# Summing a router's row blocks in PSUM by thirds of the tokens, and even static capacities, in a fused attention and mixture-of-experts kernel

## The chip, the cores and the metric

One Trainium2 chip, one of its cores. The metric is device microseconds of one execution, lower is better. The kernel before takes 606.49 us (median of three runs, 604.68 to 609.28).

## The reference, cut to what matters

Windowed attention for 8 batches, 8 heads, 576 positions and head size 64 gives a table x of 4608 tokens by 512 features. A two-level router then picks one of 16 experts for each token, and the token goes through that expert's two layers:

```python
g_logits = x @ w_group                 # 4 groups
g_idx = np.argmax(g_logits, axis=1)
...
    e_logits = xg @ w_expert[g]        # 4 experts in each group
    e_idx = np.argmax(e_logits, axis=1)
    ...
            h = np.maximum(xg[mask_e] @ w1[g, e], 0.0)     # 512 -> 1024
            ye = h @ w2[g, e]                              # 1024 -> 512
            out[tok_idx] = combined[:, None] * ye
```

So the router needs 20 numbers for each token: 4 group logits and 16 expert logits, each a sum over 512 features. On this input the reference sends 442, 405, 368, 301, 299, 298, 291, 284, 265, 264, 255, 255, 242, 238, 213 and 188 tokens to the sixteen experts, in the order in which the kernel ranks them.

## The kernel before, in words

**Attention.** The tokens are handled in 4 pairs of batches (1152 tokens each), and each pair in 9 steps, 36 steps in all. A step loads its queries, keys and values by DMA from SyncE's queue (tiles qb, kr, vt), computes scores on TensorE (PE; L266, L278), their maxima and differences on VectorE (DVE; L288, L289), the exponentials on ScalarE (ACT; L294), turns them (L301), multiplies by the values (tile o, L311), divides (L337, L339), stores x to DRAM and turns x into xT (L363, L365, L367). POOL (GpSimd) makes a shifted copy of the values (L125, L131). PE, ACT, DVE and SyncE run in the order in which the program writes their instructions; POOL's order is made by a planner.

**Router.** When the 9 steps of a pair are done, `route` runs for it, a piece at a time between later attention steps (`spend` with its budget). xT has the 512 features as 4 row blocks c of 128 partitions. In the kernel before, the 1152 tokens are cut into three thirds of 384. For each third, four products (one for each row block c) write four different 32-partition blocks of one PSUM tile lt_ps (L380), so the four partial sums lie under one another; the middle third is cut in two because it spans two batches. ACT copies each third to SBUF (tile lt, L387). In the next attention step, nine products, one for each 128-token tile, take a 128x128 block of lt as the stationary operand and a 128x20 matrix `sumsel` of ones and zeros as the moving one: that turns the tile and adds the four partial sums at once (tile lg_ps, L391). VectorE then finds the maxima (L396 and on), and a long chain gives each token a slot in its expert's list, ending in products into tb_ps (L521) and an addition to `tab` (L531). Float32 products on PE show as two records each, so 36 products of L391 are 72 records.

**The last pair's route** runs in the tail after the attention, in an order written out by hand (the string TAIL), between the first, early pieces of the expert layers. There `overflow`, `order` and `select` find the lists of rows, and POOL gathers rows of x for the experts (L700).

**Experts.** The experts are ranked by their number of tokens, and the rank r has a static capacity CAPS[r]: the layers are computed for that many columns, whatever the number of tokens. Parts of ranks 0 and 1 are done early (128+128 and 256 columns). For the rest, `layer1` does 8 blocks of 12 products (L750) in which the token columns are the moving operand, and `layer2` does 24 products for each tile of 128 tokens (L809) in which the weights move, 512 columns at a time; a last tile of at most 64 tokens is done in 2 groups side by side, one of at most 32 in 4. `spread` turns the gathered rows (L731). Tokens over a capacity are handled by a loop at the end of the program, once for each 128 of them, with its own load of the expert's weights; on this input it runs zero times.

Of the kernel before, what the change touches and what calls it, by code (L numbers as in the profile page):

```python
# [8 lines left out]
F32 = mybir.dt.float32  # L9
# [4 lines left out]
ALU = mybir.AluOpType  # L14
# [3 lines left out]
P = 128  # L18
B, H, S, D = 8, 8, 576, 64
# [7 lines left out]
TPB = 2 * S // P  # L27
# [9 lines left out]
CLS = S // 4  # L37
EARLY = ((0, 0, 128, 2), (0, 128, 128, 3), (1, 0, 256, 3))
AFTER = (2, 3)
CAPS = (448, 408, 368, 304, 304, 304, 296, 288, 272, 264, 256, 256, 248, 240, 216, 192)  # L40
DONE = [max([o + n for q, o, n, _ in EARLY if q == r] + [0]) for r in range(len(CAPS))]
PIECES = [(r, DONE[r], n - DONE[r]) for r, n in enumerate(CAPS)]
CMAX = max(n for _, _, n in PIECES)
# [21 lines left out]
def moe_attention_kernel(ctx, tc, q, k, v, cmask, wgate, wpack, out):  # L65
    nc = tc.nc
    pool = lambda name, bufs=1, **kw: ctx.enter_context(tc.tile_pool(name=name, bufs=bufs, **kw))
    cp = pool("cp")
    dram = pool("dram", space=bass.MemoryType.DRAM)
    psS = pool("psS", 2, space=PSUM)  # L70
    psT = pool("psT", 2, space=PSUM)
    psX = pool("psX", 1, space=PSUM)
    psR = pool("psR", 1, space=PSUM)
# [4 lines left out]
    id32 = cp.tile([P, P], F32, name="id32")  # L78
# [13 lines left out]
    sm = pool("sm", 1)  # L92
# [61 lines left out]
    upper = cp.tile([P, P], BF16, name="upper")  # L154
    wgr = cp.tile([P, 128 + NCHK], F32, name="wgr")
    wg = wgr[:, 0:128].rearrange("p (c n) -> p c n", c=4)
    sumsel = cp.tile([P, 20], F32, name="sumsel")
    pri = cp.tile([P, 4], F32, name="pri")
    base = [cp.tile([P, NE], F32, name="base0")] + [None] * NBP
    low = cp.tile([P, P], F32, name="low")  # L160
# [19 lines left out]
    def iota_of(t, pattern, base, mult):  # L180
        nc.gpsimd.iota(t, pattern=pattern, base=base, channel_multiplier=mult, allow_small_or_imprecise_dtypes=True)

    def setup(part):
        if part == 0:
            nc.vector.memset(ones, 1.0)
            nc.gpsimd.affine_select(
                out=upper, in_=ones, pattern=[[1, P]], compare_op=ALU.is_gt, fill=0.0, base=0, channel_multiplier=-1
            )
            nc.sync.dma_start(wgr, wgate)
            nc.vector.tensor_copy(sumsel, id32[:, 0:20])  # L190
            for c in range(1, 4):
                nc.vector.tensor_tensor(sumsel, sumsel, id32[:, 32 * c : 32 * c + 20], ALU.add)
            iota_of(pri, [[-1, 4]], 4, 0)
            iota_of(base[0], [[REG, NE]], 0, 0)
            iota_of(low, [[1, P]], 0, 0)
        if part == 1:
            iota_of(val[:, :, 0], [[P, NCHK]], -NTOK, 1)
            iota_of(parts[:, :, 0], [[P, NCHK]], -NTOK, 0)
            iota_of(parts[:, :, 3], [[0, NCHK]], 0, 1)
            iota_of(high, [[REG // P, NE], [1, NK4]], 0, 0)  # L200
            nc.vector.tensor_scalar(high, high, float(P), HUGE, ALU.mult, ALU.add)
            nc.vector.memset(E16, 0.0)
            nc.vector.memset(tab[:, 0], float(NTOK))
            nc.vector.memset(tab[:, 1], 0.0)
            nc.vector.memset(tab[:, 2], 2.0 * NTOK + 1.0)
            nc.vector.tensor_copy(val[:, :, 2], wgr[:, 128:])
            nc.vector.tensor_scalar(parts[:, :, 2], val[:, :, 2], R256, R256, ALU.add, ALU.subtract)
            nc.vector.tensor_tensor(parts[:, :, 5], val[:, :, 2], parts[:, :, 2], ALU.subtract)
        if part == 2:
            for t in sum(xe, []):  # L210
                nc.gpsimd.memset(t, 0.0)
            nc.sync.dma_start(xd[NTOK : NTOK + 1, :], xe[0][0][0:1, :])
        if part == 3:
            for g, t in oob.items():
                for i in range(g):
                    nc.gpsimd.memset(t[P // g * i : P // g * i + P // g], float(g * NTOK + i))
            for r in range(NE):
                nc.vector.memset(capt[:, r : r + 1], float(CAPS[r]))

# [134 lines left out]
    xT = {}  # L354
# [13 lines left out]


    def route(bp):  # L370
        lt = sm.tile([P, TPB, P], F32, name="lt")
        TPC = TPB // 3
        for i in range(3):
            ps = (psT, psT, psR)[i].tile([P, TPC * P], F32, name="lt_ps", tag="ttr"[i])
            a0 = i * TPC * P
            cuts = [a0] + [S] * (a0 < S < a0 + TPC * P) + [a0 + TPC * P]
            for a, b in zip(cuts, cuts[1:]):
                bb, s0, n = a // S, a % S, b - a
                for c in range(4):
                    nc.tensor.matmul(  # L380
                        ps[32 * c : 32 * c + 32, a - a0 : b - a0],
                        wg[:, c],
                        xT[bp][:, c, bb, s0 : s0 + n],
                        start=True,
                        stop=True,
                    )
            nc.scalar.copy(lt[:, i * TPC : i * TPC + TPC].rearrange("p t n -> p (t n)"), ps)  # L387
        yield 2
        lg_ps = psR.tile([P, TPB, 20], F32, name="lg_ps", tag="r")
        for t in range(TPB):  # L390
            nc.tensor.matmul(lg_ps[:, t], lt[:, t], sumsel, start=True, stop=True)  # L391
        n, last = TPB, bp + 1
        T = lambda nm, shape, dt=F32: sm.tile([P] + shape, dt, name=nm)
        l5 = lg_ps.rearrange("p t (r e) -> p t r e", e=4)
# [50 lines left out]
        for t in range(n):  # L445
# [4 lines left out]
                start=False,  # L450
                stop=(t == n - 1),
# [32 lines left out]
        for t0 in range(0, n, 3):  # L484
# [33 lines left out]
            for t1, lo, hv in done:  # L518
                for t in range(3):
                    for h in range(2):  # L520
# [4 lines left out]
                            start=(t1 + t + h == 0),  # L525
                            stop=(t1 + t == n - 1 and h == 1),
# [239 lines left out]
    def layer2(w, ent, cs, cap, between=lambda i: None, tail=None):  # L766
# [34 lines left out]
        if tl[-1][1] < P:  # L801
            tl.insert(0 if cap == CAPS[-1] else 1, tl.pop())
        for k, (t, n) in enumerate(tl):
# [80 lines left out]
    start = []  # L884
# [5 lines left out]
    for s in range(NT + 3):  # L890
# [13 lines left out]
        if start:  # L904
            n = start.pop()
            routes.append(route(n))
            for i, (_, _, _, pairs) in enumerate(EARLY):
                if pairs == n + 1:
                    routes.append(settle(i))
# [11 lines left out]
        if 2 <= s <= 8 and s % 2 == 0:  # L921
            setup(s // 2 - 1)
# [14 lines left out]
        if s >= 3 and (s - 3) % NJ == NJ - 1:  # L937
            bp = (s - 3) // NJ
# [122 lines left out]
    def ready():  # L1061
        cur[:] = begin(0)

    lastr = [route(NBP - 1)]
    bgq = [overflow()]
    rq = [order()]
# [138 lines left out]
```

## Time and profile before

| | us |
|---|---|
| median of three runs | 606.49 |
| profiled execution, whole | 609.38 |
| its span, first to last instruction | 607.7 |
| PE busy | 571.0 (94%) |
| DVE busy | 395.1 (65%) |
| ACT busy | 329.5 (54%) |
| POOL busy | 247.7 (41%) |

The profiled execution took 609.38 us, 2.9 us over the median of the runs. "Busy" is the union of an engine's instructions. PEld is TensorE's loading of stationary operands, which runs beside its products. The granted clock of TensorE is given as a share of full speed, so 1.00 is 2.4 GHz and 0.50 is 1.2 GHz.

### The profile page before, as it was taken

The page shows a single profiled execution, that of the slowest core. Times are in us where ns is not written, and L with a number is a line of the kernel's source. Part 1 is how long each engine was busy: PE and PEld are TensorE (multiplying, and loading weights), DVE is VectorE, ACT ScalarE, POOL GpSimd, SP SyncE. Part 2 cuts the span into 40 slices and gives each one's busy share as a digit, 9 for nine tenths or more (in the row PEclk, how much of TensorE's full clock was granted, in tenths as well). Part 3 has the DMA queues.
Part 4 walks back from the last instruction along what each step waited for, and adds up shares of the span by engine and source line. Part 5 has one row for each costly group of instructions (what it writes and reads, how often), then busy time and mean ns, then how long its engine had stood idle before and what let it go on. Part 6 is the DMA issues. An engine that isn't in the chain of part 4 may idle for free.

```text
span 607.7 us, 18716 instructions
## 1 busy us (share of the span) xinstructions
PE 571.0 (94%) x7636; PEld 400.4 (66%) x7636; DVE 395.1 (65%) x800; ACT 329.5 (54%) x658; POOL 247.7 (41%) x314
## 2 busy tenths in 40 slices
PE   5898999988879999999999999999999999999995
PEld 3665776666666668665666575666757767767873
DVE  5764874897957853774778786655755666656720
ACT  2555674675566533774465555465655756656521
POOL 4754582655726324143425151433524413413411
PEclk9999998989989999999999999999999999999999
DMA  7998796799374118676567576757668578677300
GB/s 245 298 287 262 238 277 185 237 356 335 71 250 144 51 47 318 219 259 205 183 198 223 187 229 205 226 175 232 209 211 258 180 243 275 227 233 254 103 30 29
DMA packets 47914, 127.52 MB, mean 210 GB/s; under 512 B 7224, under 2 KB 8126, under 8 KB 47826
## 3 DMA queue, kind: packets, MB, share of 16 engines
q1 hardware_dynamic: 40466, 105.31, 54.9%
q0 software_dynamic: 7360, 20.98, 9.8%
q8 instruction: 62, 1.02, 0.7%
q14 instruction: 26, 0.21, 0.1%
HBM read 107.38 MB, written 19.24 MB: 208 GB/s over the span
## 4 chain that ended last, share of the span: by engine, by line
PE 65%; issue 3%; DVE 2%; POOL 1%; ACT 1%; POOLq 0%
PE y L809 31%; PE a L750 30%; PE pt L731 3%; DVE mv L502 1%; POOL xe L700 1%; PE tb_ps L521 0%; POOL out L770 0%; PE rp L676 0%; ACT off L246 0%; DVE room L758 0%; ACT xT L367 0%; ACT ohl L247 0%; PE o L311 0%; ACT room L757 0%; DVE room L733 0%
## 5 line engine op out<-in xcount | busy, mean ns | idle before, releaser
L700 POOL DMA_INDIRECT xr<-xd,sent x80 | 96.1, 1201 | 35.2 <-issue 22.2
L809 PEld LDWEIGHTS <-hh 128*128 128x128 f16 (+10 forms) x960 | 67.5, 99 | 58.0 <-issue 2.9
L770 POOL DMA_INDIRECT out<-yr,sent x30 | 30.2, 1007 | 180.2 <-ACT yr L783 148.0
L758 DVE SCALAR_TENSOR_TENSOR hl<-a,hh 128x256 f16<-128x256 f32 (+11 forms) x136 | 57.3, 424 | 65.9 <-ACT hh L757 64.8
L757 ACT ACTIVATE hh<-a 128x256 f16<-128x256 f32 (+11 forms) x136 | 51.9, 385 | 51.9 <-PE a L750 51.2
L750 PE MATMUL a<-xh,wb1h 128*128 128x256 f16 (+6 forms) x288 | 77.0, 271 | 0.0
L750 PE MATMUL a<-xl,wb1h 128*128 128x256 f16 (+6 forms) x288 | 77.0, 271 | 0.0
L750 PE MATMUL a<-xh,wb1l 128*128 128x256 f16 (+6 forms) x288 | 77.0, 271 | 0.0
L733 DVE TENSOR_TENSOR xl<-pt,xh 128x512 f16<-128x512 f32 (+10 forms) x42 | 24.8, 594 | 73.5 <-ACT xh L732 73.5
L750 PE MATMUL a<-xh,wa1h 128*128 128x192 f16 (+7 forms) x256 | 71.2, 278 | 0.0
L750 PE MATMUL a<-xh,wa1l 128*128 128x192 f16 (+7 forms) x256 | 71.2, 278 | 0.0
L750 PE MATMUL a<-xl,wa1h 128*128 128x192 f16 (+7 forms) x256 | 71.2, 278 | 0.0
L783 ACT ACTIVATE yr<-y,cs 128x512 f32<-128x512 f32 (+3 forms) x30 | 20.6, 687 | 90.1 <-PE y L809 61.9
L750 PEld LDWEIGHTS <-wa1h 128*128 128x128 f16 x640 | 59.3, 98 | 13.4 <-issue 1.8
L750 PEld LDWEIGHTS <-wb1h 128*128 128x128 f16 x576 | 54.4, 98 | 10.0
L809 PE MATMUL y<-wb2h,hh 128*128 128x512 f16 (+6 forms) x272 | 59.7, 305 | 0.0
L809 PE MATMUL y<-wb2l,hh 128*128 128x512 f16 (+6 forms) x272 | 59.6, 304 | 0.0
L809 PE MATMUL y<-wb2h,hl 128*128 128x512 f16 (+6 forms) x272 | 59.6, 304 | 0.0
L809 PE MATMUL y<-wa2h,hh 128*128 128x512 f16 (+7 forms) x208 | 56.8, 332 | 0.0
L809 PE MATMUL y<-wa2l,hh 128*128 128x512 f16 (+7 forms) x208 | 56.6, 330 | 0.0
L809 PE MATMUL y<-wa2h,hl 128*128 128x512 f16 (+7 forms) x208 | 56.6, 330 | 0.0
L809 PEld LDWEIGHTS <-hl 128*128 128x128 f16 (+10 forms) x480 | 34.6, 99 | 25.2
(190 smaller groups left out, 1255.4 us busy)
## 6 DMA issues: line engine op xcount, KB each, us to landing
w<-wpack SPq DMA_DIRECT2D x128, 512.0 KB, 3.9
vt<-v SPq DMA_DIRECT2D x36, 260.0 KB, 4.8
qb<-q SPq DMA_DIRECT2D x36, 256.0 KB, 4.6
xd<-x SPq DMA_DIRECT2D x72, 128.0 KB, 3.9
kr<-k SPq DMA_DIRECT2D x34, 256.0 KB, 4.4
xr<-xd,sent POOLq DMA_INDIRECT x80, 4.1
kr<-k SPq DMA_DIRECT2D x4, 128.0 KB, 3.2
out<-yr,sent POOLq DMA_INDIRECT x30, 2.8
```

The costliest lines, as they stand in the source:

```text
L502: nc.vector.scalar_tensor_tensor(mv[:, t], high.rearrange("p e k -> p (e k)").unsqueeze(1).broadcast_to([P, 6, NE * NK4]), hl[:, 1, t0 + t ...
L700: nc.gpsimd.indirect_dma_start(out=xr[:, 256 * h : 256 * h + 256], out_offset=None, in_=xd[0:known].rearrange("n (h c) -> (n h) c", h=2), ...
L731: nc.tensor.transpose(pt[:, c, 0:n], xr[0:n, c * P : c * P + P], id32[0:n, 0:n])
L733: nc.vector.tensor_tensor(xl[:, :, t * P : t * P + n], pt[:, :, 0:n], xh[:, :, t * P : t * P + n], ALU.subtract)
L750: nc.tensor.matmul(a[:, 0:cap], ww[:, c * FF + f * P : c * FF + f * P + P], xx[:, c, 0:cap], start=(i == 0), stop=(i == len(mm) - 1),)
L757: nc.scalar.activation(hh[:, f, 0:cap], a[:, 0:cap], AF.Relu)
L758: nc.vector.scalar_tensor_tensor(hl[:, f, 0:cap], a[:, 0:cap], 0.0, hh[:, f, 0:cap], ALU.max, ALU.subtract)
L770: ins = nc.gpsimd.indirect_dma_start(out=out.rearrange("n (g c) -> (n g) c", g=g), out_offset=bass.IndirectOffsetOnAxis(ap=at, axis=0), in ...
L783: nc.scalar.activation(yr[0:n, :], yp[0:n, :], AF.Copy, scale=cs[0:n, t : t + 1])
L809: nc.tensor.matmul(yp[P // g * j : P // g * j + n, 0 : DM // g], h[:, f, t * P : t * P + n], ww[:, f * DM + DM // g * j : f * DM + DM // g ...
```

## The change

It does two things. In `route`, the three thirds now go to three 32-partition blocks of one PSUM tile, and the four row blocks c are added in PSUM by accumulation, so one copy of 96 partitions takes the place of three of 128. A product of the next stage then turns three token tiles (one of each third) at once, with a 96x60 selection matrix `sel3` in place of the 128x20 `sumsel`: three products in place of nine. And the capacities go from multiples of eight to the next even number; twelve of them shrink, by 48 columns in all.

```diff
-CAPS = (448, 408, 368, 304, 304, 304, 296, 288, 272, 264, 256, 256, 248, 240, 216, 192)
+CAPS = (442, 406, 368, 302, 300, 298, 292, 284, 266, 264, 256, 256, 242, 238, 214, 188)
...
-    sumsel = cp.tile([P, 20], F32, name="sumsel")
+    sel3 = cp.tile([P, 3, 20], F32, name="sel3")
...
-            nc.vector.tensor_copy(sumsel, id32[:, 0:20])
-            for c in range(1, 4):
-                nc.vector.tensor_tensor(sumsel, sumsel, id32[:, 32 * c : 32 * c + 20], ALU.add)
+            for j in range(3):
+                nc.vector.tensor_copy(sel3[:, j], id32[:, 32 * j : 32 * j + 20])
...
     def route(bp):
-        lt = sm.tile([P, TPB, P], F32, name="lt")
         TPC = TPB // 3
-        for i in range(3):
-            ps = (psT, psT, psR)[i].tile([P, TPC * P], F32, name="lt_ps", tag="ttr"[i])
-            a0 = i * TPC * P
-            cuts = [a0] + [S] * (a0 < S < a0 + TPC * P) + [a0 + TPC * P]
-            for a, b in zip(cuts, cuts[1:]):
-                bb, s0, n = a // S, a % S, b - a
-                for c in range(4):
+        lt = sm.tile([3 * 32, TPC * P], F32, name="lt")
+        ps = psT.tile([P, TPC * P], F32, name="lt_ps", tag="t")
+        for c in range(4):
+            for j in range(3):
+                a0, a1 = j * TPC * P, (j + 1) * TPC * P
+                cuts = [a0] + [S] * (a0 < S < a1) + [a1]
+                for a, b in zip(cuts, cuts[1:]):
+                    bb, s0 = a // S, a % S
                     nc.tensor.matmul(
-                        ps[32 * c : 32 * c + 32, a - a0 : b - a0],
+                        ps[32 * j : 32 * j + 32, a - a0 : b - a0],
                         wg[:, c],
-                        xT[bp][:, c, bb, s0 : s0 + n],
-                        start=True,
-                        stop=True,
+                        xT[bp][:, c, bb, s0 : s0 + b - a],
+                        start=(c == 0 and a == a0),
+                        stop=(c == 3 and b == a1),
                     )
-            nc.scalar.copy(lt[:, i * TPC : i * TPC + TPC].rearrange("p t n -> p (t n)"), ps)
+        nc.scalar.copy(lt, ps[0 : 3 * 32])
         yield 2
         lg_ps = psR.tile([P, TPB, 20], F32, name="lg_ps", tag="r")
-        for t in range(TPB):
-            nc.tensor.matmul(lg_ps[:, t], lt[:, t], sumsel, start=True, stop=True)
+        for t in range(TPC):
+            nc.tensor.matmul(
+                lg_ps.rearrange("p (j t) e -> p j t e", t=TPC)[:, :, t],
+                lt[:, t * P : t * P + P],
+                sel3[0 : 3 * 32],
+                start=True,
+                stop=True,
+            )
```

## Rows read from the trace of the kernel before

**Rows 1.** Busy time by stage (start:end, length, then each engine's busy time), clock, DMA.
```profile
core 0: us, PE busy (x) PEld busy (x) DVE busy (x) ACT busy (x) POOL busy (x), PEclk, DMA share, GB/s
...
20.00:180.00 160.00, 139.46 (x3788) 104.37 (x3787) 117.48 (x252) 96.87 (x247) 86.48 (x138) 0.95 0.80 249
180.00:230.00 50.00, 47.74 (x433) 33.43 (x433) 33.71 (x94) 24.84 (x57) 20.12 (x26) 1.00 0.28 94
...
300.00:400.00 100.00, 100.00 (x776) 65.21 (x775) 72.79 (x150) 53.10 (x90) 37.27 (x33) 1.00 0.65 205
```

**Rows 2.** Chain that ended last: start, us, what; first layer at 304 and 264 columns.
```profile
295.58 6.20 PE a L750 x48
...
455.17 5.40 PE a L750 x48
```

**Rows 3.** Timeline of PE, 300 to 350: turning of a full tile and of 48 rows.
```profile
313.32 0.60 PE L731 MATMUL pt<-id,xr 128*128 128x128 f32 x4
...
317.28 0.45 PE L731 MATMUL pt<-id,xr 48*128 48x48 f32 x4
```

**Rows 4.** Groups by line (busy, mean ns): the router's products, loads and copies.
```profile
L380 PE MATMUL lt_ps<-xT,wgr 128*32 128x384 f32 (+1 forms) x128 | 9.4, 410 | 1.1 <-issue 0.9
L391 PE MATMUL lg_ps<-sumsel,lt 128*128 128x20 f32 x72 | 9.3, 275 | 0.0
L391 PEld LDWEIGHTS lg_ps<-sumsel,lt 128*128 128x128 f32 x72 | 8.9, 201 | 0.4
...
L387 ACT COPY lt<-lt_ps 128x384 f32<-128x384 f32 x12 | 5.7, 479 | 4.4 <-PE lt_ps L380 4.1
```

**Rows 5.** Line L380 alone, 182.5 to 182.7 and 183.3 to 183.6: min/median/max ns.
```profile
L380 PE MATMUL lt_ps<-xT,wgr x8: 486/498/511, 182.3 to 182.7; 128*32 128x384 f32 x8
...
L380 PE MATMUL lt_ps<-xT,wgr x16: 326/326/327, 183.0 to 183.5; 128*32 128x192 f32 x16
```

**Rows 6.** Timeline of the last pair's route, 180 to 212: PE, ACT, DVE and POOL.
```profile
182.33 2.15 PE L380 MATMUL lt_ps<-xT,wgr 128*32 128x384 f32 x32
...
185.76 2.14 PE L391 MATMUL lg_ps<-sumsel,lt 128*128 128x20 f32 x18
...
189.24 0.35 ACT L419 ACTIVATE df<-df 128x180 f32<-128x180 f32 x1 [1.56 <-DVE oh L402]
...
190.84 1.00 POOL L700 DMA_INDIRECT xe<-xd,ente  x1 [0.30 <-issue]
...
192.12 0.35 POOL L422 TENSOR_TENSOR df<-df 128x90 f32<-128x90 f32 x1
...
194.37 0.22 DVE L475 RECIPROCAL val<-se 128x9 f32<-128x9 f32 x1 [1.27 <-POOL se L428]
```

**Rows 7.** Waits of PE, 20 to 165 us: us in total, times, longest.
```profile
PE o L311 <- issue: 8.0, 11, 1.9
PE t L301 <- ACT p L294: 7.0, 5, 2.0
```

**Rows 8.** Line L391 alone in three stretches: length, PE busy, PEld busy, clock, DMA.
```profile
98.10:101.50 3.40, 1.51 (x14) 1.51 (x14) 1.00 0.72 217
145.90:149.30 3.40, 2.19 (x18) 2.08 (x18) 1.00 1.02 359
60.50:63.90 3.40, 2.21 (x18) 2.03 (x18) 1.00 0.87 280
```

**Rows 9.** All lines, the stretches after two of those (columns as in rows 1).
```profile
101.50:108.30 6.80, 6.80 (x115) 5.20 (x115) 3.42 (x8) 1.81 (x6) 2.97 (x10) 0.50 0.49 132
...
149.30:152.70 3.40, 3.40 (x70) 2.55 (x70) 3.26 (x7) 2.38 (x5) 2.44 (x4) 0.50 0.46 157
```

**Rows 10.** DVE's making of sumsel: ns min/median/max, first and last start.
```profile
L192 DVE TENSOR_TENSOR sumsel<-sumsel,id x3: 178/180/536, 18.1 to 18.5; 128x20 f32<-128x20 f32 x3
L190 DVE COPY sumsel<-id x1: 296/296/296, 17.7 to 17.7; 128x20 f32<-128x20 f32 x1
```

## Prediction

> **What bounds the kernel now.** I read the busy time by stage first. In the expert layers PE is busy for 100.00 of 100 us at full clock [rows 1], so there every nanosecond that PE is spared shortens the kernel, and nothing else does. In the attention no engine is full: PE 139.46 of 160 us, DVE 117.48, DMA at 0.80 [rows 1]; steps are paced by several things in turn, and the waits of PE say which: 8.0 us in which the profile names no releaser and 7.0 us for ACT's exponentials [rows 7]. A spared microsecond of PE there passes on only in part. Between them, in the tail at 180 to 230 us, PE lacks 2.26 us of work [rows 1], and the timeline shows what is late: POOL gathers rows until 191.84, then sums the router's exponentials from 192.12, and DVE waits for that until 194.37 [rows 6].
>
> **Capacities.** 448-442, 408-406 and so on add up to 48 columns less. A column costs layer 1 96 products (8 blocks of 12). Rank 3 at 304 columns takes 6.20 us for 48 products, 129.2 ns each, and rank 9 at 264 columns 5.40 us, 112.5 ns [rows 2]: 16.7 ns for 40 columns, 0.417 ns a column, with no step between them. So 48 x 96 x 0.417 = 1.92 us. The sizes shown are multiples of eight; none at 2 or 4 is. If PE rounded up to eight the gain would be 0, and no rounding can make it a loss, so the bounds are 0 and 1.92; I take 1.92: 264 is no multiple of 16 and still lies on the line, so no coarser rounding shows, and nothing hints at a finer one. Layer 2 moves weights, not tokens, and no last tile crosses 64 or 32 tokens, so the groups and the number of products stay: 0. Turning the rows: four products over 48 columns end 0.15 us earlier than over 128 [rows 3], 1.9 ns a column, 0.1 us for 48. The evictions on ACT and DVE shrink too, covered by a PE that is full; with that cover gone they would only help. The number of gathers and their 128 rows each, and the scatters, stay. **Experts: -2.0 us.**
>
> **Making sel3.** One copy and three additions on DVE, about 1.2 us, become three copies of 20 columns [rows 10]. It lies at 18 us, 40 us before L391 first uses it [rows 8], and shifts nothing that waits: 0; uncovered it would be a gain of some 0.4.
>
> **First products of the route (L380).** Per pair before: two passes (records) for each product. A pass over 384 columns lasts 486 ns and one over 192 columns 326 ns [rows 5]: 160 ns for 192 columns, so 0.32 us of streaming for 384, 0.16 for 192, and 0.17 of latency. Four row blocks side by side in four 32-column tiles of the array: 2 x (0.32 + 0.16 + 0.16 + 0.32) + 0.17 = 2.09 us, and the timeline has 2.15 [rows 6]: the four do run side by side, with 128 records of 410 ns in 9.4 us [rows 4]. After: three tiles are used, each streams its third four times: 4 x 2 x 0.32 + 0.17 = 2.73 us, **+0.6 us per pair**. The new order puts the two pieces of the middle third, which share a tile, behind one another; no row shows two products of one tile in succession. Lower bound +0.6 (a tile can't stream less); the upper bound is a strict order of starts, worked out as a rival below, +2.8. I take +0.6, since in rows 5 and 6 a second pass that waits for its own tile does not hold back the other tiles.
>
> A page of the Trainium skill says otherwise: "TensorE: Matmul & The Clock Gate", Part 3 (Packing small matmuls), has products start and end strictly in program order, only weight loads being pulled ahead. By that rule a product's second pass, in the same tile, would have held back the next product in the kernel before too, and its 2.15 us would have been over 4. The trace doesn't agree with that; by that rule the sum would be the third rival's.
>
> **Copy (L387).** Three of 479 ns become one over the same 384 columns: ACT -0.96 us per pair. ACT is at 96.87 of 160 us in the attention [rows 1], and the copy is read a step later, so 0 on the path; the one copy starts later (it needs the last product), covered by that step. In the tail it would end at about 182.33 + 2.73 + 0.5 = 185.6; between L380 and L391 PE has 1.3 us of early expert products (184.48 to 185.76 [rows 6]), which would then last until 186.3: still covered.
>
> **Second products (L391).** Nine become three, 18 records become 6. 18 records take 2.14 us [rows 6], 0.11 us apart, which is set by the load of 128 float32 columns (8.9 of 9.3 us busy [rows 4]). The moving part grows from 20 to 60 columns, 40 x 0.83 = 33 ns by rows 5, hidden behind the load or added to it: 6 x 0.11 to 6 x 0.145 + 0.15 = 0.8 to 1.0 us. **-1.2 us per pair** (1.1 to 1.3).
>
> **What of the route reaches the end.** Per pair PE gets 0.6 back. The last pair: L391 ends at about 187.3 instead of 187.9 and L419 at 189.0 instead of 189.59, but POOL is gathering until 191.84 in either case [rows 6]; the 2.5 us there are the cover, and the saving is idle time before the next sums: 0. Were that cover gone, 0.6 would count. The three pairs in the attention: between 0 (all absorbed by the loads) and 1.8 us (PE-bound throughout); half, **-0.9 us**, since about half of PE's waits are of a kind that moves with the work (ACT p) [rows 7].
>
> **Sum.** -2.0 - 0.9 = -2.9 us against a profiled execution of 609.38. That execution is 2.9 us above the median of the runs, so I set the sum against the median: 606.5 - 2.9 = **603.5 us**.
>
> **Rivals.** (1) *The clock.* After L391 filled 1.51 and 2.19 of 3.4 us [rows 8] the clock fell to 0.50 (1.2 GHz) for 6.8 and 3.4 us [rows 9]. L391 is mostly loading, with 20 columns moving. With a third of it there the two falls may not come: half of 6.8 and of 3.4 us, 5.1 us of PE, passed on by a half or in full, 603.5 - 2.5 to 603.5 - 5.1: 598.4 to 601.0. Against: after the first pair's L391, 2.21 of 3.4 us, no fall came [rows 8], and PE's waits around the other two remain.
> (2) *The route's saving is absorbed.* The loads pace the attention (DMA 0.80 [rows 1]) and PE waits a little longer for them: 606.5 - 2.0 = 604.5; with columns rounded up as well 606.5, no change.
> (3) *Slower: strict order in the array.* If passes started only in program order, a row block would take 0.32 (first third) + 0.16 + 0.16 + 0.16 (its second pass and the middle pieces) + 0.32 = 1.12 us, L380 4 x 1.12 + 0.5 = 5.0 us, +2.8 per pair, -1.2 for L391: +1.6 net. Three pairs passed on in full give +4.8; the last one is still covered by the 2.5 us. With the experts 606.5 + 4.8 - 2.0 = 609.3. It decides from about +1.9 us per pair in L380 on, where it outweighs the experts. Against it: rows 4 to 6.
> (4) *One token too many.* Eight capacities now equal the reference's counts. Should the chip's rounding send one more token to one of them, the overflow loop runs once, with eight weight chunks and a 128-token pass of both layers: layer 1 at least 96 x 56 ns (128 columns at 0.417 and about 2) and layer 2 one full tile's 5.2 us, over 10 us beside its loads: above 616. Two capacities equalled their counts already (368 and 264), and the loop ran zero times.
>
> **How the numbers follow.** Forecast as summed 0.50; (1) 0.20; (2) 0.20; (3) 0.08; (4) 0.02. About 1% (6 us) is what a measurement of this kernel can tell from no change. Faster by over 1% (below 600.4) is most of (1) and a corner of the first: 0.20. Slower by over 1% (above 612.6) is (4) and the worst of (3), with a POOL order newly planned: 0.05. Within: 0.75. Range 599.0 to 607.5: from the middle of (1) to no change with the spread of the runs (604.68 to 609.28).
>
> **What would show it.** L380 at 32 records and about 2.7 us per pair (5 for rival 3); L391 at 6 records and under 1.0; one copy of 96x384; rank 3's layer 1 at 302 columns, 128.3 ns a product; PE still without idle time in the expert layers, their length shorter by 2.0 us; POOL's sums of the last pair still starting right after its gathers. Wrong if the expert stretch keeps its length, if the clock's falls after the second and third pair vanish and the time with them, or if the attention ends later than before.

## The result, and the profile after

The changed kernel takes **602.77 us** (median of 20 runs, 599.08 to 607.40), the kernel before, on the same chip, 607.36 us (20 runs, 604.10 to 614.36): ratio 0.992, 95% interval 0.9898 to 0.9943, so 3.5 to 6.2 us less. Forecast were 603.5 us and -2.9. The profiled execution took 603.11 us (span 601.4, mean clock 0.986, the one before 609.38, 607.7 and 0.982).

Busy time by stage, columns as in [rows 1]:

```profile
20.00:180.00 160.00, 139.19 (x3808) 104.67 (x3809) 118.82 (x266) 96.02 (x244) 87.32 (x141) 0.96 0.81 259
180.00:230.00 50.00, 47.20 (x409) 33.03 (x404) 31.43 (x82) 23.89 (x52) 20.56 (x25) 1.00 0.29 91
300.00:400.00 100.00, 100.00 (x765) 64.31 (x764) 72.12 (x145) 54.28 (x90) 34.42 (x30) 1.00 0.66 205
```

At this grain nothing seems to have happened: PE is as busy in the attention as before and has all of 100 us in the experts. The gain is in *when* the stages end. The chain that ended last (start, us, what) has the experts' first full-width layer at 209.91 in the kernel before and at 205.61 in the changed one:

```profile
209.91 10.48 PE a L750 x96
```

```profile
205.61 10.48 PE a L755 x96
...
290.69 6.16 PE a L755 x48
...
318.04 6.12 PE a L755 x48
...
449.20 5.40 PE a L755 x48
...
516.66 9.92 PE a L755 x96
```

From there to the end of the span it is 601.4 - 205.61 = 395.8 us, before 607.7 - 209.91 = 397.8: **-2.0 us in the experts**. PE's own work got 2.3 us shorter. Its last product, before and changed, is

```profile
601.02 0.38 PE L809 MATMUL y<-wb2l,hh 128*128 128x512 f16 x1
```

```profile
594.45 0.38 PE L814 MATMUL y<-wb2l,hh 128*128 128x512 f16 x1
```

and ends 391.5 us after the start of that layer before, 389.2 in the changed kernel. What follows it (the last result and its scatter) lasts 6.6 us here and 6.3 before, so that 2.0 are left; in the experiments below it lasts 6.0 (e1) to 6.6 us (f4). The ranks at 302, 300, 264 and 242 columns take 128.3, 127.5, 112.5 and 103.3 ns a product, on the line of [rows 2] (129.2 at 304). The other **4.3 us** of these two executions were gained before 205.61.

The route's two groups of products by tile (min/median/max ns, first and last start):

```profile
L379 PE MATMUL lt_ps<-xT,wgr x128: 326/416/510, 55.7 to 180.2; 128*32 128x384 f32 x64, 128*32 128x192 f32 x64
L386 ACT COPY lt<-lt_ps x4: 476/476/476, 58.9 to 180.6; 96x384 f32<-96x384 f32 x4
```

```profile
L390 PEld LDWEIGHTS lg_ps<-sel,lt x24: 186/192/192, 61.9 to 182.4; 96*128 96x128 f32 x24
L390 PE MATMUL lg_ps<-sel,lt x24: 272/275/320, 61.9 to 182.4; 96*128 96x60 f32 x24
```

One copy for three, 24 records for 72. The tail's timeline (start, us), with the last pair's route in it:

```profile
177.76 2.82 PE L379 MATMUL lt_ps<-xT,wgr 128*32 128x384 f32 x32
177.89 0.35 DVE L536 TENSOR_TENSOR tab<-tab,tb_ps 128x192 f32<-128x192 f32 x1
...
180.61 0.48 ACT L386 COPY lt<-lt_ps 96x384 f32<-96x384 f32 x1 [2.97 <-PE lt_ps L379]
...
181.39 0.28 ACT L762 ACTIVATE room<-a 128x128 f16<-128x128 f32 x1 [0.30 <-PE a L755]
...
181.86 0.83 PE L390 MATMUL lg_ps<-sel,lt 96*128 96x60 f32 x6
...
182.87 0.29 DVE L763 SCALAR_TENSOR_TENSOR room<-a,room 128x128 f16<-128x128 f32 x1 [0.88 <-ACT room L762]
183.08 1.22 DVE L637 SCALAR_TENSOR_TENSOR wb1l<-w,wb1h 128x1024 f16<-128x1024 f32 x1
184.21 0.34 DVE L401 TENSOR_REDUCE mx<-lg_ps 128x45 f32<-128x180 f32 x1
...
186.77 1.00 POOL L705 DMA_INDIRECT xe<-xd,ente  x1 [0.30 <-issue]
...
187.79 0.36 POOL L427 TENSOR_TENSOR df<-df 128x90 f32<-128x90 f32 x1
...
190.06 0.22 DVE L480 RECIPROCAL val<-se 128x9 f32<-128x9 f32 x1 [0.89 <-POOL se L433]
```

L379 takes 2.82 us ([rows 6]: 2.15), L390 0.83 (2.14). The addition to `tab` (L536) closes the third pair's route and serves below as the mark where the attention ends: 177.89 here, 182.46 before. The kernel before has the mark and the last pair's maxima at

```profile
182.46 0.34 DVE L531 TENSOR_TENSOR tab<-tab,tb_ps 128x192 f32<-128x192 f32 x1
...
188.11 0.34 DVE L396 TENSOR_REDUCE mx<-lg_ps 128x45 f32<-128x180 f32 x1
```

From the mark to the reciprocal it is 12.17 us here and 194.37 - 182.46 = 11.91 before, so the tail gave nothing and lost 0.3.

### The profile page after: what moved, and what is told of

It is laid out like the page before. It is cut to its first block, busy times and chain, and to the rows that moved or that the text cites. A ratio compares the mean times of both kernels' runs of the same rounds, so it can differ in the third digit from the quotient of the medians.

```text
span 601.4 us, 18614 instructions
## 1 busy us (share of the span) xinstructions
PE 563.5 (94%) x7588; PEld 395.9 (66%) x7588; DVE 392.8 (65%) x799; ACT 326.2 (54%) x650; POOL 247.4 (41%) x314
## 4 chain that ended last, share of the span: by engine, by line
PE 65%; issue 3%; DVE 2%; POOL 1%; ACT 1%; POOLq 0%
PE y L814 31%; PE a L755 30%; PE pt L736 3%; DVE mv L507 1%; POOL xe L705 1%; PE tb_ps L526 0%; POOL out L775 0%; PE rp L681 0%; ACT off L245 0%; DVE room L763 0%; PE o L310 0%; ACT xT L366 0%; ACT ohl L246 0%; ACT room L762 0%; DVE room L738 0%
## 5 line engine op out<-in xcount | busy, mean ns | idle before, releaser
L814 PEld LDWEIGHTS <-hh 128*128 128x128 f16 (+14 forms) x960 | 67.2, 99 | 57.7 <-issue 2.7
L755 PE MATMUL a<-xh,wb1h 128*128 128x256 f16 (+7 forms) x288 | 76.6, 270 | 0.0
L755 PE MATMUL a<-xh,wb1l 128*128 128x256 f16 (+7 forms) x288 | 76.5, 269 | 0.0
L755 PE MATMUL a<-xl,wb1h 128*128 128x256 f16 (+7 forms) x288 | 76.5, 269 | 0.0
L755 PE MATMUL a<-xh,wa1h 128*128 128x186 f16 (+7 forms) x256 | 70.7, 277 | 0.0
L755 PE MATMUL a<-xh,wa1l 128*128 128x186 f16 (+7 forms) x256 | 70.7, 276 | 0.0
L755 PE MATMUL a<-xl,wa1h 128*128 128x186 f16 (+7 forms) x256 | 70.7, 276 | 0.0
L814 PE MATMUL y<-wb2h,hh 128*128 128x512 f16 (+7 forms) x272 | 59.7, 305 | 0.0
L814 PE MATMUL y<-wb2l,hh 128*128 128x512 f16 (+7 forms) x272 | 59.6, 304 | 0.0
L814 PE MATMUL y<-wb2h,hl 128*128 128x512 f16 (+7 forms) x272 | 59.5, 304 | 0.0
```

The costliest lines, as they stand in the source:

```text
L755: nc.tensor.matmul(a[:, 0:cap], ww[:, c * FF + f * P : c * FF + f * P + P], xx[:, c, 0:cap], start=(i == 0), stop=(i == len(mm) - 1),)
L814: nc.tensor.matmul(yp[P // g * j : P // g * j + n, 0 : DM // g], h[:, f, t * P : t * P + n], ww[:, f * DM + DM // g * j : f * DM + DM // g ...
```

## Experiments

Times are medians. The first four kernels ran beside the kernel before at 606.61 us (29 runs), e5 to e8 on a chip on which the same kernel before takes 619.97 (18 runs), the last four beside 606.28 (34 runs); only ratios are compared across chips.

**e1: the capacities alone.** The kernel before with the new CAPS.

> The kernel before with the even capacities alone. If a column costs 0.417 us of layer 1 per expert whatever its parity, the expert stretch (first 256-column product to the last instruction, 397.9 us before) gets 1.9 to 2.0 us shorter, and the median falls by about 2.0 us (0.33%); the attention keeps its length within its spread. If PE rounds columns up to eight, the stretch keeps its length and the median its time. If to four (302 as 304, 298 as 300, 442 as 444), 22 of the 48 columns come back: about -1.1 us.

604.85 us, ratio 0.9974 (0.9943 to 1.0006). The interval takes in no change, but the stages tell: the experts' full-width stretch, counted from its first product, is 395.4 us where the kernel before has 397.9, and PE's last product ends 389.2 us after the first full-width layer of the chain, as in the changed kernel, where the kernel before has 391.5. The columns are worth 2.3 us; the 0.2 to 0.3 us more or less in the stretches of e1 and of the changed kernel lie behind PE's last product. (Rounded up to multiples of four, 16 of the 48 columns would come back and not 22, which leaves 1.3 us; that is excluded too.)

**e2: the router alone.** The changed kernel with the old CAPS.

> The changed router with the old capacities. By the forecast's sum -0.9 us (0 to -1.8) from PE's own time in the three routes of the attention; by the theory that the clock's falls after the second products go, -2.5 to -5 us and a higher granted clock than the kernel before in the same call; by the theory that the loads absorb it all, 0 within 0.7. The expert stretch stays at 397.9 us in each.

602.69 us, ratio 0.9930 (0.9899 to 0.9961): -3.9 us, the larger part, and it all lies before the mark (176.26): from the mark to the fourth pair's addition to `tab` it is 19.66 us, in the kernel before 19.42.

**e3: e2 with nine second products again**, each of 20 columns, from the one lt tile.

```diff
-        for t in range(TPC):
+        for t in range(TPB):
...
-                lg_ps.rearrange("p (j t) e -> p j t e", t=TPC)[:, :, t],
-                lt[:, t * P : t * P + P],
-                sel3[0 : 3 * 32],
+                lg_ps[:, t],
+                lt[:, t % TPC * P : t % TPC * P + P],
+                sel3[0 : 3 * 32, t // TPC],
```

> The router of e2, but again nine second products of 20 columns for a pair (96 rows, 18 records, about 2.1 us of PE), on the accumulated and copied thirds. PE then has 0.6 us per pair more than the kernel before. If the thinner second products are what gains, this loses all of e2's gain, and 0 to 2 us more: 0 to +2 us against the kernel before, with the clock falling after the second products as before. If the single copy on ACT, or POOL's newly planned order, is what gains, it keeps e2's time.

608.91 us, ratio 1.0027 (0.9995 to 1.0059); line L390 alone (PE and PEld busy, clock, as in [rows 8]):

```profile
54.46:70.00 15.54, 2.19 (x18) 2.08 (x18) 0.69 (x2) 0.94 0.70 200
```

2.19 us a pair for 0.88: 3 x 1.31 = 3.9 us of PE in the attention cost 6.2 us. The single copy, the freed PSUM tiles and the order of POOL are as in e2, so they aren't where the gain is: without the shorter second products the new router is at best even.

**e4: e2 with the loops over thirds and row blocks exchanged**, so that a third's products follow one another.

```diff
-        for c in range(4):
-            for j in range(3):
-                a0, a1 = j * TPC * P, (j + 1) * TPC * P
+        for j in range(3):
+            a0, a1 = j * TPC * P, (j + 1) * TPC * P
+            for c in range(4):
```

> The router of e2 with the loops of the first products exchanged: all products of a third, which share one 32-column tile, before the next third. If products of different tiles start out of order however far behind they are written, the 32 records of a pair still take about 2.7 us. If starts keep the written order, the thirds follow one another and they take 3 x 2.56 + 0.17 = 7.8 us. In between: the queue looks ahead only some products.

616.53 us (one run). L379 alone, first pair:

```profile
54.46:60.53 6.07, 6.07 (x32) 2.82 (x32) 0.00 (x0) 1.00 0.85 269
```

6.07 us for the same 32 records that take 2.82 in the changed order; without any overlap they would take 7.8. In these two orders tiles run side by side only as far as the products of different tiles stand near each other in the program. The mark moves by 186.28 - 176.26 = 10.0 us for 3 x 3.25 = 9.8 us of PE. Two executions of one attention can differ by 1.8 us in the mark (182.46 in the kernel before, 180.65 in e1), so this says: PE's time comes through about in full, not by half. In the tail (mark to fourth addition 22.6 us) the fourth 3.25 comes through as 2.95: POOL's cover is used up there.

**e5 and e6: what fills PE, time or idle columns?** e2 with sixteen dense bfloat16 products of 180 columns ahead of the three second products (e5), or with each second product done three times (e6).

```diff
+        flat = lg_ps.rearrange("p t e -> p (t e)")
+        for _ in range(16):
+            nc.tensor.matmul(flat, idb, masks.rearrange("p m c -> p (m c)")[:, 0 : TPB * 20], start=True, stop=True)
```

```diff
-        for t in range(TPC):
+        for t in [t for t in range(TPC) for _ in range(3)]:
```

> The router of e2 with 16 scratch products of 180 bfloat16 columns (16 x 77 ns = 1.2 us per pair) put ahead of the three second products and overwritten by them: PE's time of the nine products is back, but as dense streaming. If e2 gained by PE's time, the fill costs 3 x 1.2 = 3.7 us against e2, about 606.5, as much as e6. If e2 gained by a clock that falls less, the fill costs little against e2 (0 to 1 us), or half of e6's loss.

> The router of e2 with each of the three second products done three times into the same place: 18 records, 1.3 us of PE more per pair, nearly all of it loading. By PE's time alone +3.9 us against e2, about 606.5. If low activity also brings the clock down, more than that: e3 lost 6.2 us to e2 with the same 18 records, so about 608.9 and a granted clock as in e3.

Ratios 1.0049 (1.0019 to 1.0079) and 1.0089 (1.0056 to 1.0123): both lose what e2 had gained, and the intervals overlap. The chip was another one, so they were repeated beside e2 (below).

**e7: POOL's gathers later in the tail.**

```diff
-    "R0w0wr0rrrrrrrrrrr1rrrr0rr1r1rr1r1rr1rrB1w12w1ww112w2w2w2w2O2O2O2O2O2O"
+    "R0w0wr0rrrrrrrErrrr1rrrr0rr1r1rr1r1rr1rrB1w12w1ww112w2w2w2w2O2O2O2O2O2O"
...
-    run(eq, 100)
```

> The changed kernel, with POOL's six gathers for the third early piece issued after POOL's sums of the last pair's route instead of ahead of them. If those gathers are what the sums wait for in the tail, the reciprocal comes about 1.2 us earlier after the third addition to tab, the stretch from the third to the fourth addition falls from 19.7 to about 18.4 us, and the median by about 1.2 us to 601.5. If the chain on VectorE is as late, it stays. If the late gathers then hold up the turning of the third early piece, it gets longer.

Ratio 0.9862 (0.9824 to 0.9900), but this tests nothing: POOL's planner put the gathers where they had been, the first of them 1.77 us after the mark as in the changed kernel (178.08 for 176.31; 179.66 for 177.89). POOL does the same 262 operations in the same order, so in effect it is the changed kernel on that chip. There its stages run otherwise, though: mark to fourth addition takes 23.73 us for 19.69, and POOL's sums wait for ACT, the gathers being done 0.6 us earlier:

```profile
187.01 0.48 POOL L427 TENSOR_TENSOR df<-df 128x90 f32<-128x90 f32 x1 [0.61 <-ACT df L424]
```

In the experts from 230 to 500 us PE lacks 3.3 of 270 us, where the changed kernel's first profile lacks none. So single stages of e5 to e8 aren't set beside those of the other runs, and why the change gains 8.8 us on that chip and 4.6 on the others stays open. That the gathers are the cover rests on e4 and on the tail's rows.

**e8: exact capacities**, eight of them odd.

```diff
-CAPS = (442, 406, 368, 302, 300, 298, 292, 284, 266, 264, 256, 256, 242, 238, 214, 188)
+CAPS = (442, 405, 368, 301, 299, 298, 291, 284, 265, 264, 255, 255, 242, 238, 213, 188)
```

> The changed kernel with every capacity at the count itself, odd ones too (405, 301, 299, 291, 265, 255, 255, 213): 8 columns less. If columns cost 0.417 us each in layer 1 at any parity, the expert stretch falls by 0.33 us and the product at 301 columns takes 127.9 ns. If odd widths round up to even, the product at 301 takes as long as at 302 and nothing changes. If odd float16 rows slow PE's reading, it gets longer.

Slower: 637.2 us, ratio 1.0274 (1.0235 to 1.0312). The waits of PE from 500 to 600 us (line waited for, us, times, longest):

```profile
PE pt L736 <- DMA xr<-xd,sent: 21.8, 2, 11.1
```

The products aren't the cause: layer 1's mean is 273 ns at 255 columns and 272 at 256, 277 at 265 and 276 at 264 (what one odd column gains or costs can't be told at this grain). POOL's timeline has it:

```profile
503.28 1.03 POOL L775 DMA_INDIRECT out<-yr,sent  x1 [9.01 <-ACT yr L788]
508.93 2.58 POOL L775 DMA_INDIRECT out<-yr,sent  x1 [4.63 <-DVE cs L662]
511.82 1.59 POOL L705 DMA_INDIRECT xr<-xd,sent  x1 [0.30 <-PE a L755]
...
538.62 1.02 POOL L775 DMA_INDIRECT out<-yr,sent  x1 [21.18 <-ACT yr L788]
544.22 2.57 POOL L775 DMA_INDIRECT out<-yr,sent  x1 [4.58 <-ACT yr L788]
547.10 1.43 POOL L705 DMA_INDIRECT xr<-xd,sent  x1 [0.30 <-PE a L755]
```

The two experts of 255 tokens scatter a last tile of 127 rows (508.93, 544.22): 2.6 us to issue in place of 1.0, and the gathers queued behind land late. The chain of waits:

```profile
547.10 19.50 DMA xr<-xd,sent
```

By stretch (columns as in [rows 1]), behind PE's last product (it ends at 520.92) in the first of the two waits:

```profile
521.00:523.00 2.00, 0.00 (x0) 0.00 (x0) 0.39 (x1) 0.00 (x0) 0.00 (x0) 1.00 0.93 268
...
525.00:531.00 6.00, 0.00 (x0) 0.00 (x0) 0.00 (x0) 0.00 (x0) 0.00 (x0) 0.50 0.09 39
531.00:532.00 1.00, 0.33 (x2) 0.36 (x3) 0.00 (x0) 0.00 (x0) 0.00 (x0) 0.50 0.06 25
```

From 525 on the DMA engines are 0.06 to 0.09 busy, one to one and a half of 16, at 25 to 39 GB/s; 127 rows of 512 float32 are 260 KB, about 10 us at 25 GB/s, which is the wait (PE idle for 10.76 us up to 531.67). The Trainium skill, "DMA: Bandwidth & Descriptors", section "Why a DMA increments its semaphore by 16 and not by 1", has the rule: a transfer runs on the largest number of engines, up to 16, that divides the slowest dimension of both its sides, some direct copies excepted, and it names 127 partitions as a case for one. The trace agrees. The smaller odd tiles of e8 (85 rows: 1.11 us on POOL) held up no product. The two waits, 21.8 us, are most of the 26 us by which e8 is behind e7 on the same chip. The prediction costed the scatters at nothing without looking at their row counts; with the even capacities that held: the new ones of 114 and 86 rows took POOL 1.16 and 1.46 us, and no product waited.

**f1 to f4: both fillings, the router alone and the whole change on one chip.**

> The router's change alone, again, as the anchor for the two fillings on this same chip. Theory (PE's time in the route comes through nearly in full): ratio to the kernel before 0.990 to 0.996, as the 0.993 of its first run. Rival (the first run was luck of a chip): 0.997 to 1.001.

> The router's change alone, and ahead of each pair's three second products sixteen bfloat16 products of 180 columns into the same PSUM tile, which are overwritten: about as much PE time as the change saves, but with columns in motion. Theory (PE's time counts, whatever fills it): slower than the router alone by 3 to 6 us, as slow as the filling by loads within 2 us. Rival (the clock: second products that are mostly loads pull it down, and a dense filling doesn't): within 2 us of the router alone, and over 3 us faster than the filling by loads.

> The router's change alone, with each of the three second products done three times (18 records in place of 6, about 2.2 us a pair, mostly loads of the stationary operand). Both theories: slower than the router alone by 3 to 6 us; the theory of PE's time has the dense filling equally slow, the rival of the clock has this one over 3 us slower than the dense filling.

> The changed kernel beside the router's change alone on one chip. If the two parts add up, it is faster than the router alone by the 1.9 us of the 48 columns (1.0 to 2.8); if the new scatters of 114, 110 and 86 rows (rows that no power of two divides) cost something, by less than 1.

| kernel | us | ratio (95%) | second products and filling, us a pair | mean clock of the runs |
|---|---|---|---|---|
| before | 606.28 | | 2.14 to 2.68 | 0.987 |
| f1, router alone | 603.11 | 0.9953 (0.9920 to 0.9987) | 0.88 | 0.988 |
| f2, dense filling | 608.21 | 1.0033 (1.0005 to 1.0061) | 2.06 | 0.990 |
| f3, repeated | 609.13 | 1.0040 (1.0008 to 1.0073) | 2.22 | 0.988 |
| f4, changed kernel | 601.57 | 0.9926 (0.9898 to 0.9954) | 0.88 | 0.990 |

Dense and mostly loading fillings cost the same, +5.1 and +6.0 us over f1, and neither lowers the clock against f1 over 11 or 12 runs each (standard error 0.001). The theory of PE's time holds, the clock's doesn't. f4 is 1.5 us under f1 (1.9 expected): the two parts add up, and the change as made is the fastest kernel measured here.

## Why the prediction was right or wrong

**Capacities, right.** -2.0 forecast; -2.3 in PE's work and -2.0 in the stretch to the end of the span. The cost of a column holds at even widths that are no multiple of four too.

**First products, right.** 2.82 us where 2.73 was forecast. (In the attention single pairs took up to 3.6 us at full clock, as the kernel before took up to 2.65 for 2.15.) The third rival, strict order, is refuted, but e4's 6.07 us shows that tiles overlap over a limited distance only. No row of before could show that, since there four tiles took turns product by product; the change's order, with one pair of one tile in succession at most, stayed within it.

**Second products, right.** 0.83 to 0.88 us, forecast 0.8 to 1.0; -1.3 a pair, forecast -1.2.

**Copy and sel3, nothing, as forecast.** e3 has both and no gain.

**Last pair, the right 0 by a wrong path.** The step said that L391 would end earlier in the tail and the gain then wait for POOL. But the maxima don't wait for it: they start 184.21 - 177.89 = 6.3 us after the mark, where in the kernel before it was 188.11 - 182.46 = 5.65, since on DVE they stand behind `room` (182.87) and the weight split L637 (183.08), and those wait for ACT's `room`, which waits for the early expert product that PE does behind L379. L379's 0.67 us more goes down that chain, L390's 1.3 us less doesn't enter it; e3, with 2.19 us in L390, has its maxima at 6.3 us too. So this pair's route came 0.7 us *later*, and POOL's gathers, which end at 187.77, hid that: its sums start right behind them here (187.79) and behind them and one short MEMSET before, 9.90 us after the mark here, 192.12 - 182.46 = 9.66 before. The 0.3 us lost are POOL's.

**Three pairs in the attention, "half, -0.9 us": the step that failed.** The mechanism (PE gets 0.6 us a pair back) was right; the share of it that is passed on, one half, was mis-sized. Measured are -3.9 (e2) and -3.2 us (f1), where even passing on in full gives 3 x 0.64 = 1.9. The step took PE's waits (8.0 and 7.0 us, [rows 7]) for slack that takes up half of what PE is spared. The stretch from 20 us to the mark shows what they are. Kernel before, changed kernel, e3 and e4, in that order (columns as in [rows 1]):

```profile
20.00:182.46 162.46, 141.51 (x3822) 106.27 (x3824) 118.47 (x257) 98.40 (x251) 86.48 (x138) 0.95 0.80 250
```

```profile
20.00:177.89 157.89, 137.08 (x3783) 103.05 (x3784) 116.89 (x256) 96.02 (x244) 86.39 (x138) 0.96 0.82 259
```

```profile
20.00:185.14 165.14, 143.76 (x3824) 109.20 (x3824) 117.35 (x256) 95.57 (x245) 85.68 (x138) 0.94 0.78 247
```

```profile
20.00:186.28 166.28, 146.31 (x3815) 106.39 (x3802) 117.54 (x255) 96.24 (x245) 85.76 (x138) 0.96 0.77 247
```

Length less PE busy is 20.95, 20.81, 21.38 and 19.97 us: the wait is about the same, whatever PE does. The same view of the other kernels, with the part of the busy time lost to the clock (the sum over stretches of 1 us of PE's busy time times what its clock lacks of 1.00) taken apart:

| kernel | mark, us | PE idle | lost to clock | busy without it |
|---|---|---|---|---|
| before | 182.46 | 21.0 | 8.4 | 133.2 |
| e1, old router | 180.65 | 21.0 | 8.5 | 131.1 |
| changed | 177.89 | 20.8 | 6.4 | 130.6 |
| e2, new router | 176.26 | 20.4 | 4.9 | 131.0 |
| f1, new router | 175.22 | 20.3 | 4.7 | 130.2 |
| f4, changed | 175.60 | 22.1 | 1.5 | 131.9 |
| f2, dense | 177.68 | 19.3 | 3.4 | 135.0 |
| f3, repeated | 182.63 | 21.8 | 6.4 | 134.5 |
| e3, nine products | 185.14 | 21.4 | 9.9 | 133.8 |
| e4, thirds in turn | 186.28 | 20.0 | 6.4 | 139.9 |

Idle time is 19.3 to 22.1 us in all ten; the mark follows PE's busy time. That is shown; it refutes the second rival (absorbed by the loads). In the last column the old router has 133.2 and 131.1 us, the new one 130.2 to 131.9 (mean 130.9), so a single profile is good to about 1 us either way; over that mean f2, f3, e3 and e4 lie by 4.1, 3.6, 2.9 and 9.0 us, where their edits add 3.5, 4.0, 3.9 and 9.8. The fourth rival, one token too many, didn't come: e1 gains.

**First rival, the clock, mostly not.** No fall follows the second products in the changed kernel: the second pair's end at 101.3 us, and the stretch behind them that stood at 0.50 in [rows 9] is at full clock; but others fall in its place (columns as there):

```profile
101.50:108.30 6.80, 6.80 (x222) 5.25 (x221) 6.06 (x18) 4.16 (x12) 3.61 (x10) 1.00 0.79 234
...
155.10:158.50 3.40, 3.40 (x83) 2.32 (x85) 3.17 (x7) 1.12 (x4) 2.57 (x4) 0.50 0.36 82
165.30:172.10 6.80, 6.22 (x101) 5.32 (x102) 2.96 (x8) 3.12 (x11) 0.00 (x1) 0.50 0.73 250
```

Nor do the falls come back with the loads: in e3 and f3, with 18 records again, the clock is full for over 10 us behind the second products of each of the three pairs. In single executions the clock weighs much: the 4.6 us between the marks of before and after are 1.9 us of clock, 2.5 of other PE time and 0.1 of idle time, and f4 lost 1.5 us to it where the changed kernel's first profile lost 6.4. Over all runs it hardly differs: mean clock 0.987 for before (29 and 34 runs), 0.990 for e2, 0.988 for f1. 0.001 of the clock is some 0.6 us of 600, so the clock gave about 0.5 to 1.8 us of the router's gain, with a standard error of about 0.7, and f2 and f3 show no tie to the second products.

**What stays open.** Time times clock, averaged over the runs, falls by 2.3 (e2) and 2.9 us (f1) where PE was spared 1.9, and rises by 5.9 (f2) and 6.0 (f3) over f1 for 3.5 and 4.0 us of PE, by 4.3 (e3) over e2 for 3.9. All five lie above one for one, by 0.4 to 2.4 us, with errors of about 0.8 each. In the profiles it can only lie ahead of the mark: behind it those of e2, f1, f2, f3 and e3 agree within 0.03 us up to the fourth addition (19.66 to 19.69 us) and within 0.05 us in PE's work on the experts. That the route's PE time is passed on in full is shown; why rather more than that arrives isn't, and no run here tells.

**The range.** Its lower end, 599.0, was called the middle of the first rival; the middle of 598.4 to 601.0 is 599.7. That the sum came within 0.7 us of the measured time is partly luck: the medians fell by 4.6 us and not by 2.9, and the forecast was set against a median of three runs, 606.5, where twenty runs give 607.4.

## What to carry to other kernels

Idle time of the busiest engine is slack only if it shrinks when that engine gets more work: here 21 us of waits stayed 21 us whether PE had 1.9 us less or 10 us more, so a saving there counts in full though no engine is full by the averages. When static sizes are trimmed, list the row counts that the scatters and gathers get: two scatters of 127 instead of 128 rows cost more than all the trimmed columns gave.

## What the runs showed of the hardware that was not expected

- Products into different 32-column tiles of PE overlap only over a limited distance in program order: 32 records over three tiles take 2.82 us with the tiles in turn and 6.07 (e4) with each tile's eight or sixteen records together. How far the overlap reaches wasn't measured.
- A scatter of 127 rows took POOL 2.6 us and then ran at 25 to 39 GB/s with 0.06 to 0.09 of the DMA engines (e8), and a gather issued behind it landed after up to 19.5 us; 128 rows take POOL 1.0 us.
- One and the same kernel takes 606 to 607 us on two chips and 620 on another, with a mean clock of 0.987 and 0.982. The clock is not the whole of it: on the slower chip PE has idle time in the experts (3.3 us in e7 from 230 to 500 us) where it has none on the others.
